# Pooled attention and a token/channel mixer in one kernel: every unit in program order on VectorE and ScalarE, with the q block transposes first in each unit

## The chip, the cores and the metric

The kernel runs on one core of one Trainium2 chip. The metric is the device time of one execution in microseconds. "The span" is the time from the first to the last instruction of the profiled execution; it is 1.7 to 1.9 us shorter than the time of the same execution.

A core has engines that run side by side, each through its own list of instructions: TensorE (PE in the profile, PEld for its weight loads), VectorE (DVE), ScalarE (ACT) and GpSimd (POOL). In the kernel before they are busy for 286.7, 178.4, 99.5 and 133.6 us of a span of 325.3. They meet at semaphores; TensorE's longest wait there for another engine is 14.4 us.

## The reference

```python
# attention over pooled keys: q, k, v are [8 batches, 8 heads, 576, 64], float32
k_p = k.reshape(B, H, 72, 8, D).mean(axis=3)        # 576 keys -> 72
v_p = v.reshape(B, H, 72, 8, D).mean(axis=3)
attn = softmax(q @ k_p.T / sqrt(D))
x = (attn @ v_p), heads side by side                # [8, 576, 512]
# mixer
h  = relu(x.T @ w_tok1) @ w_tok2                    # over the tokens, 576 -> 256 -> 576
u  = x + h.T
h2 = relu(u @ w_ch1) @ w_ch2                        # over the channels, 512 -> 1536 -> 512
return u + h2                                       # float32
```

## The kernel before

The kernel has a head (batch 0's attention) and then nine "units". Unit n runs the channel mixer of batch n on TensorE, 48 matmuls with `w_ch1` (the "ch1" phase) and 48 with `w_ch2`, and slips the attention and the token mixer of batch n+1 between them. The matmuls are a Python generator with 48 stops, called slots; a table says which step of batch n+1 is traced at which slot. Unit 8 does the leftover rows of all batches.

```python
def unit_steps(n, st):                              # 48 slots, 0.43 us of TensorE each
    for m in range(NM):                             # NM = 12, slots 0 to 23
        ps = ps_one.tile([P, 512], FP32, name="p1")
        for kk in range(4):
            nc.tensor.matmul(out=ps, lhsT=w_ch1[...], rhs=uT[:, kk, :], ...)        # L412
            if kk == 1:
                yield
        if m % 4 != 3 or n == 0:
            nc.scalar.activation(out=GT[:, m, :], in_=ps, func=AF.Relu)             # L417
        else:
            nc.vector.tensor_scalar(out=GT[:, m, :], in0=ps, ..., op0=ALU.max)      # L419
        yield
    ...                                             # slots 24 to 47: w_ch2 (L424), output o (L429)

FIRST = {1: "K0", 3: "u0", 5: "K1", 6: "u1", 8: "q0 u2", 10: "kpT0", 11: "u3", ...}          # unit 0
LATER = {0: "Q0", 1: "kpT", 3: "Q1", 6: "e0", 8: "o0", 10: "e1", 12: "o1", 14: "e2", 16: "o2",
         18: "e3", 20: "o3", 23: "av0", 25: "av1", ...}                                      # units 1 to 7
```

The steps that matter are these.

- `Q0`, `Q1`: four VectorE block transposes each of batch n+1's q (tile `qb` to `qD`, L253), from batch 2 on. They need the transfer of `qb`.
- `kpT`: eight TensorE transposes of the pooled keys and a VectorE copy to `kD` (L211).
- `e0`, `o0` to `e3`, `o3`: the scores (TensorE L271, from `qD` and `kD`) and their exponentials on ScalarE (L277).
- `av0` to `av4`: attention times v (TensorE L293), normalised by VectorE into `x` (L311); then the token mixer (L339, L354) whose results VectorE evicts into `u` (L355).

PSUM, the matmuls' output memory, is split in pools. `ps_one`, three buffers of 128 x 512 float32, serves the ch1 and ch2 tiles and the u tiles alike. A buffer is free when its tile has been evicted (the 14.4 us above are a ch1 tile that waits for the eviction of a u tile).

```python
ps_one = ctx.enter_context(tc.tile_pool(name="ps_one", bufs=3, space=bass.MemoryType.PSUM))
ps_two = ctx.enter_context(tc.tile_pool(name="ps_two", bufs=2, space=bass.MemoryType.PSUM))   # scores, av
```

Last, who decides the order. Outside `tc.manual_schedule` the framework's scheduler chooses the order of each engine's list at compile time. Inside, the engines named run in the order of tracing.

```python
with tc.manual_schedule(engines={PE, POOLE}):
    batches = [batch_steps(b) for b in range(B)]
    with tc.manual_schedule(engines={DVE, ACT}):
        ...                                        # head, loads
        unit(0, FIRST)
    for n in range(1, B + 1):                      # VectorE and ScalarE left to the scheduler
        unit(n, LATER)
```

The softmax here doesn't subtract the row's maximum and nothing guards it: scores larger than these inputs give would overflow.

Of the kernel before, what the change touches and what calls it, by code (L numbers as in the profile page):

```python
# [12 lines left out]
PE = mybir.EngineType.PE  # L13
POOLE = mybir.EngineType.Pool
DVE = mybir.EngineType.DVE
ACT = mybir.EngineType.Activation
# [3 lines left out]
def kernel(  # L20
# [14 lines left out]
    nc = tc.nc  # L35
    B, H, S, D = q.shape
    P = 128
# [25 lines left out]
    w_tok1 = singles.tile([P, 6, DT], BF16)  # L63
    w_tok2 = singles.tile([P, 2, S], BF16)
    w_tok2t = singles.tile([P, 2, 2, P], BF16)
# [6 lines left out]
    kTs = [singles.tile([P, 2, H * SP], BF16, name=f"kTs{i}") for i in range(2)]  # L72
    kps = [singles.tile([SP, H, 2, 2, D // 2], BF16, name=f"kps{i}") for i in range(2)]
# [4 lines left out]
    def load(b):  # L78
        if b >= B:
            return  # L80
        kr = raw.tile([SP, H, POOL, D], BF16, name="kr")
        vr = raw.tile([SP, H, POOL, D], BF16, name="vr")
        qb = raw.tile([P, HP, BR * D + D], BF16, name="qb")
        if b < BY_PE:
            nc.vector.memset(qb[:, :, BR * D:], 0.0)
        loaded[b] = (kr, vr, qb)

        def q_in(a0, a1):
            return q[b, 2 * a0:2 * a1].rearrange("(a l) (p r) d -> (l p) a (r d)", l=2, r=BR)

        def kv(t, src, h0, h1):
            nc.gpsimd.dma_start(out=t[:, h0:h1].rearrange("j h i d -> j h (i d)"),
                                in_=src[b, h0:h1].rearrange("h (j i) d -> j h (i d)", i=POOL))

        if b == 0:
            for a in range(2):
                nc.sync.dma_start(out=qf[:, a:a + 1, :], in_=q_in(a, a + 1))
            loaded["q23"] = q_in
            kv(kr, k, 0, HP)
            kv(kr, k, HP, H)  # L100
            make_identity(nc, ident)
            kv(vr, v, 0, HP)
            kv(vr, v, HP, H)
        else:
            kv(kr, k, 0, H)
            if b < BY_PE:
                nc.gpsimd.dma_start(out=qb[:, :, 0:BR * D], in_=q_in(0, HP))
            else:
                for ph in range(2):
                    nc.gpsimd.dma_start(  # L110
                        out=qb[ph * 64:(ph + 1) * 64, :, 0:BR * D],
                        in_=q[b].rearrange("(a l) (j u r) d -> u (l j) a (r d)", l=2, u=2, r=BR)[ph])
            kv(vr, v, 0, H)

    def load_tok():
        nc.gpsimd.dma_start(out=f2, in_=moe_w_tok2.rearrange("(c p) n -> p c n", p=P))
        w = moe_w_tok1.rearrange("(p r) n -> p r n", r=BR)
        for half in range(2):
            rows = slice(half * BP, (half + 1) * BP)
            nc.gpsimd.dma_start(out=w_tok1[rows, 0:4, :],  # L120
                                in_=w[:, 0:8, :].rearrange("p (c u) n -> p c u n", u=2)[:, :, half])
        for half in range(2):
            rows = slice(half * BP, (half + 1) * BP)
            nc.gpsimd.dma_start(out=w_tok1[rows, 4 + half, :], in_=w[:, 8, :])

    def permute_tok2():
        src = f2.rearrange("t m (p r) -> t m r p", r=BR)
        dst = w_tok2.rearrange("t m (r p) -> t m r p", p=BP)
        for m in range(2):
            nc.gpsimd.tensor_copy(out=dst[:, m], in_=src[:, m])  # L130
        for half in range(2):
            nc.gpsimd.tensor_copy(out=w_tok2t[:, :, half, half * BP:(half + 1) * BP], in_=w_tok2[:, :, 8 * BP:S])

    def load_ch1():
        for g in range(3):
            cols = slice(g * 512, (g + 1) * 512)
            nc.gpsimd.dma_start(out=w_ch1[:, :, cols], in_=moe_w_ch1[:, cols].rearrange("(c p) n -> p c n", p=P))

    def load_ch2():
        for g in range(3):  # L140
            nc.gpsimd.dma_start(out=w_ch2[:, 4 * g:4 * g + 4, :],
                                in_=moe_w_ch2[g * 512:(g + 1) * 512, :].rearrange("(c p) n -> p c n", p=P))
# [261 lines left out]
    def unit_steps(n, st):  # L404
# [16 lines left out]
        for c in range(4):  # L421
# [8 lines left out]
            for half in range(2):  # L430
# [6 lines left out]
    HEAD = """c0 c1 d8 q0 d3 q1 d7 kpool0 d2 kpT0 d2 o0 c2 e0 kpool1 o1 e1 c3 q2 kpT1 d1 q3 d1 o2 d2 e2 vpool0 o3 vpool1  # L437
              e3 d3 av1 av0 av2 d2 av3 at_0 at_2 av4 at_1 at_3 d2 at_4 X0 X1 X2 A0 A1 A2 X3 A3 d3"""
    FIRST = {1: "K0", 3: "u0", 5: "K1", 6: "u1", 8: "q0 u2", 10: "kpT0", 11: "u3", 12: "q1", 13: "o0", 14: "e0",
             16: "kpT1 V0", 17: "o1", 18: "e1", 19: "q2", 20: "o2 V1", 21: "e2", 22: "q3", 23: "o3", 24: "e3",  # L440
             25: "av0", 26: "av1", 27: "av2", 28: "av3", 29: "av4", 31: "at0", 32: "at1", 34: "U0", 35: "U1",
             36: "t0 U2", 38: "t1 U3", 39: "U4", 40: "t2", 42: "t3", 46: "t4"}
    LATER = {0: "Q0", 1: "kpT", 3: "Q1", 6: "e0", 8: "o0", 10: "e1", 12: "o1", 14: "e2", 16: "o2",
             18: "e3", 20: "o3", 23: "av0", 25: "av1", 27: "av2", 29: "av3", 31: "av4", 33: "at0", 34: "at1",
             37: "u0", 38: "u1", 39: "t0", 40: "u2", 41: "t1", 42: "u3", 43: "u4 t2", 45: "t3", 47: "t4"}
    warm = singles.tile([P, 512], BF16)

    def head(s):
        if s[0] == "d":
            ps = ps_tr.tile([P, 512], FP32, name="pt")  # L450
            for _ in range(int(s[1:])):
                nc.tensor.matmul(out=ps, lhsT=warm[:, 0:P], rhs=warm, start=True, stop=True)  # L452
        elif s[0] == "c":
            a = int(s[1:])
            if a == 1:
                for i in range(2, HP):
                    nc.scalar.dma_start(out=qf[:, i:i + 1, :], in_=loaded["q23"](i, i + 1))
            (nc.vector.tensor_copy if a % 2 else nc.scalar.copy)(out=batches[0][2]["qb"][:, a, 0:BR * D], in_=qf[:, a, :])
        else:
            batches[0][1][s]()  # L460

    def unit(n, at):
        side = {}
        if n + 1 < B:
            load(n + 2)
            batches[n + 1][0]()
            side = batches[n + 1][1]
        for i, _ in enumerate(unit_steps(n, batches[n][2] if n < B else None)):
            for s in at.get(i, "").split() if side else []:
                if (n + 1) % 2 or s not in ("u4", "t4"):  # L470
                    (batches[0][1][s] if n == 0 and s[0] == "u" else side[s.lower() if s[0] == "U" else s])()

    with tc.manual_schedule(engines={PE, POOLE}):
        batches = [batch_steps(b) for b in range(B)]
        with tc.manual_schedule(engines={DVE, ACT}):
            nc.vector.memset(warm, 0.0)
            load(0)
            nc.vector.memset(kTs[0][D:P, 0, :], 0.0)
            nc.vector.memset(kTs[0][0:D, 1, :], 0.0)
            nc.vector.memset(w_tok1[:, 4:6, :], 0.0)  # L480
            nc.vector.memset(w_tok2t, 0.0)
            load_tok()
            load_ch1()
            permute_tok2()
            load(1)
            load_ch2()
            batches[0][0]()
            for s in HEAD.split():
                head(s)
            nc.vector.memset(kTs[1][D:P, 0, :], 0.0)  # L490
            nc.vector.memset(kTs[1][0:D, 1, :], 0.0)
            for kp in kps:
                nc.vector.memset(kp, 0.0)
            unit(0, FIRST)
        for n in range(1, B + 1):
            unit(n, LATER)

# [29 lines left out]
```

## Time and profile before

The median is 327.54 us (326.58 to 327.65). The page's second part cuts the span into 40 slices of 8.1 us; a digit is the busy share in tenths, PEclk is the granted TensorE clock in tenths of full speed, and DMA is the busy share of the core's 16 transfer engines.

```profile
PE   8699503859999899899988998999999999999994
DVE  4357207999725972697269717972465166322121
PEclk9999955986999999999999999999999999999999
DMA  7999997091691977918901210121023011204114
```

The sixth slice (40.7 to 48.8 us) is empty on TensorE and on VectorE while the transfer engines are busy. The clock record has TensorE at half clock (0.50 in the windows view) from 40.7 to 57.7 us and again from 71.4 to 78.2 us. To see what that is worth, cut the span where each unit's first ch1 matmul starts. In the windows view the columns are the stretch, its length, busy time of each engine with the number of instructions, granted clock, transfer share and GB/s.

```profile
29.00:90.30 61.30, 39.62 (x231) 19.14 (x230) 41.54 (x71) 14.74 (x26) 27.66 (x27) 0.81 0.77 116
90.30:121.70 31.40, 29.68 (x195) 15.14 (x194) 20.33 (x38) 10.35 (x18) 30.38 (x28) 1.00 0.76 134
...
219.40:248.60 29.20, 29.18 (x197) 15.38 (x195) 14.34 (x28) 10.36 (x18) 0.00 (x0) 1.00 0.16 37
248.60:278.90 30.30, 30.27 (x203) 15.99 (x202) 14.90 (x29) 10.36 (x18) 0.00 (x0) 1.00 0.15 35
```

Units 5 and 6 (the last two lines) keep TensorE busy throughout: 29.2 and 30.3 us are the floor of a unit, the second with the leftover rows of two batches. Unit 0 takes 61.3. The waits of TensorE (engine, line, what it waited for; total us, times, longest) name the reason, and the waits of VectorE name the reason behind it:

```profile
PE p L412 <- DVE u L355: 14.4, 1, 14.4
PE p L293 <- DVE x L311: 7.1, 8, 1.3
PE p L339 <- DVE xt L311: 2.0, 4, 0.7
```

```profile
DVE qD L253 <- DMA qb<-in_q_dram: 15.4, 1, 15.4
```

The timeline of VectorE in unit 0 (start, us, engine, line, operation, out<-in, count, idle time before it and who ended it) shows the scene:

```profile
33.65 1.21 DVE L148 TENSOR_TENSOR t<-kr 72x1024 f32<-72x1024 bf16 x1
50.30 0.81 DVE L253 STREAM_TRANSPOSE qD<-qb 64x576 bf16<-64x576 bf16 x1 [15.44 <-DMA qb<-in_q_dram]
51.02 0.64 DVE L149 TENSOR_TENSOR t<-t 72x512 f32<-72x512 f32 x1
51.69 0.81 DVE L253 STREAM_TRANSPOSE qD<-qb 64x576 bf16<-64x576 bf16 x1
52.53 0.69 DVE L155 TENSOR_TENSOR kp<-t 72x512 bf16<-72x512 f32 x1
53.14 1.28 DVE L355 TENSOR_TENSOR u<-p,x 128x512 bf16<-128x512 f32 x2
```

A transpose of batch 2's q, which unit 1 will need, stands in unit 0 between two halves of batch 1's key pooling. Its transfer lands at 50.3 us. Everything behind it waits too, the u evictions at 53.14 included, although their inputs had been there for 14 to 17 us. TensorE's next ch1 tile finds no free buffer; its last matmuls before the hole are those of a u tile:

```profile
38.88 0.59 PE L354 MATMUL p<-AT,w_tok 128*128 128x512 bf16 x2 [0.69 <-ACT GT L417]
53.87 1.01 PE L412 MATMUL p<-uT,w_ch 128*128 128x512 bf16 x2 [14.40 <-DVE u L355]
```

In unit 2, and likewise in units 1, 3 and 4, VectorE mixes transposes of a later batch with the x evictions:

```profile
136.44 0.81 DVE L253 STREAM_TRANSPOSE qD<-qb 64x576 bf16<-64x576 bf16 x1
137.28 0.69 DVE L311 TENSOR_TENSOR x<-p,den 128x512 bf16<-128x512 f32 x1
137.89 0.20 DVE L305 RECIPROCAL den<-p 128x8 f32<-128x8 f32 x1
138.00 0.78 DVE L253 STREAM_TRANSPOSE qD<-qb 64x576 bf16<-64x576 bf16 x1
```

```profile
138.03 0.43 PE L293 MATMUL p<-vp,ex 72*128 72x65 bf16 x8 [1.29 <-DVE x L311]
```

This is the 1.29 us wait of L293 on x; there is one such in each of these units.

### The profile page before, as it was taken

Reading aid. Unit: us, or ns where it says so; the run is one execution under the profiler, and the core shown is the slowest. Engines: PE = TensorE matmul, PEld = TensorE weight load, DVE = VectorE, ACT = ScalarE, POOL = GpSimd, SP = SyncE. Lnnn points to the kernel's source line nnn. Section 1 sums busy time; section 2 is a strip of 40 time slices with the busy share of each in tenths; the row PEclk is TensorE's granted clock in tenths of the full one; section 3 lists DMA queues with packets and bytes.
Section 4 is the critical chain, followed back from the end, with each engine's and each line's share of the span. In section 5 each row is a group of like instructions: output and inputs, shape, how many; then the busy total and the mean of one; then the engine's idle time right before and its main releaser. Section 6 shows DMA issues by size and latency. Waiting matters only on the chain.

```text
span 325.3 us, 4486 instructions
## 1 busy us (share of the span) xinstructions
PE 286.7 (88%) x1796; PEld 145.9 (45%) x1796; DVE 178.4 (55%) x332; ACT 99.5 (31%) x176; POOL 133.6 (41%) x136
## 2 busy tenths in 40 slices
PE   8699503859999899899988998999999999999994
PEld 3465201434554355445544554355545554444441
DVE  4357207999725972697269717972465166322121
ACT  2453301820056007400650074007402810330500
POOL 7292200199999999967725481500000000000000
PEclk9999955986999999999999999999999999999999
DMA  7999997091691977918901210121023011204114
GB/s 152 216 206 203 207 174 110 0 144 37 100 199 22 153 160 102 149 34 128 189 0 32 67 32 0 34 64 34 0 57 75 0 34 42 57 0 97 32 34 97
DMA packets 26868, 28.25 MB, mean 87 GB/s; under 512 B 4960, under 2 KB 21728, under 8 KB 26848
## 3 DMA queue, kind: packets, MB, share of 16 engines
q0 software_dynamic: 20512, 17.35, 36.1%
q1 hardware_dynamic: 6048, 10.03, 12.4%
q10 hardware_dynamic: 288, 0.59, 0.6%
q8 instruction: 14, 0.23, 0.3%
q14 instruction: 6, 0.05, 0.0%
HBM read 35.85 MB, written 9.44 MB: 139 GB/s over the span
## 4 chain that ended last, share of the span: by engine, by line
PE 70%; DVE 19%; DMA 7%; ACT 1%; issue 1%
PE p L412 25%; PE p L424 23%; DVE qD L253 8%; DMA qb<-in_q_dram 7%; PE p L354 5%; PE p L271 4%; DVE x L311 4%; PE p L339 4%; PE pt L452 3%; PE pt L364 2%; PE p L293 1%; DVE vp L158 1%; DVE o L429 1%; DVE den L305 1%; DVE xt L311 1%
## 5 line engine op out<-in xcount | busy, mean ns | idle before, releaser
L424 PE MATMUL p<-w_ch,GT 128*128 128x512 bf16 x432 | 112.8, 383 | 0.0
L412 PE MATMUL p<-uT,w_ch 128*128 128x512 bf16 x384 | 97.1, 383 | 15.8 <-DVE u L355 14.4
L417 ACT ACTIVATE GT<-p 128x512 bf16<-128x512 f32 x84 | 49.6, 591 | 105.1 <-PE p L412 93.0
L412 PEld LDWEIGHTS <-w_ch 128*128 128x128 bf16 x432 | 41.7, 98 | 53.1 <-issue 16.6
L424 PEld LDWEIGHTS <-GT 128*128 128x128 bf16 x432 | 39.0, 98 | 39.2 <-issue 4.1
L253 DVE STREAM_TRANSPOSE qD<-qb 64x576 bf16<-64x576 bf16 x48 | 39.0, 813 | 25.2 <-DMA qb<-in_q_dram 15.4
L419 DVE TENSOR_SCALAR GT<-p 128x512 bf16<-128x512 f32 x24 | 16.4, 684 | 60.2 <-PE p L412 60.2
L277 ACT ACTIVATE ex<-p 72x576 bf16<-72x576 f32 (+1 forms) x64 | 41.2, 646 | 10.9 <-PE p L271 10.2
L149 POOL TENSOR_TENSOR t<-t 72x512 f32<-72x512 f32 x24 | 30.4, 1268 | 1.9
L429 DVE TENSOR_TENSOR o<-p,u 128x512 f32<-128x512 f32 x32 | 21.9, 686 | 10.4 <-PE p L424 10.2
L293 PE MATMUL p<-vp,ex 72*128 72x65 bf16 x320 | 17.5, 197 | 9.4 <-DVE x L311 7.1
L148 POOL TENSOR_TENSOR t<-kr 72x1024 f32<-72x1024 bf16 x12 | 25.5, 2126 | 0.1
L148 POOL TENSOR_TENSOR t<-vr 72x1024 f32<-72x1024 bf16 x12 | 25.4, 2116 | 0.0
L355 DVE TENSOR_TENSOR u<-p,x 128x512 bf16<-128x512 f32 x32 | 21.9, 688 | 6.3 <-PE p L354 6.3
L293 PEld LDWEIGHTS <-ex 72*128 72x128 bf16 x320 | 14.5, 100 | 23.5 <-DVE x L311 16.2
L330 ACT ACTIVATE AT<-p 128x512 bf16<-128x512 f32 x8 | 4.8, 597 | 66.0 <-PE p L339 63.3
L311 DVE TENSOR_TENSOR x<-p,den 128x512 bf16<-128x512 f32 x30 | 20.5, 682 | 0.7
L110 POOL DMA_DIRECT2D qb<-in_q_dram x12 | 7.6, 634 | 30.6 <-DVE qD L253 26.8
L354 PE MATMUL p<-AT,w_tok 128*128 128x512 bf16 x64 | 19.0, 379 | 0.9 <-ACT GT L417 0.9
L271 PE MATMUL p<-qD,kD 128*72 128x288 bf16 x96 | 19.6, 286 | 0.0
L158 POOL TENSOR_TENSOR vp<-t 72x256 bf16<-72x256 f32 x12 | 8.7, 725 | 22.3 <-PE p L293 21.6
L271 PEld LDWEIGHTS <-kD 128*72 128x72 bf16 x96 | 10.8, 113 | 10.6
(90 smaller groups left out, 243.9 us busy)
## 6 DMA issues: line engine op xcount, KB each, us to landing
out_dram<-o SPq DMA_DIRECT2D x72, 128.0 KB, 2.4
kr<-in_k_dram POOLq DMA_DIRECT2D x7, 576.0 KB, 9.1
vr<-in_v_dram POOLq DMA_DIRECT2D x7, 576.0 KB, 14.1
qb<-in_q_dram POOLq DMA_DIRECT2D x12, 288.0 KB, 9.6
w_ch<-in_moe_w_ch_dram POOLq DMA_DIRECT2D x6, 512.0 KB, 12.9
qf<-in_q_dram SPq DMA_DIRECT2D x2, 288.0 KB, 3.1
kr<-in_k_dram POOLq DMA_DIRECT2D x2, 288.0 KB, 7.8
vr<-in_v_dram POOLq DMA_DIRECT2D x2, 288.0 KB, 11.1
```

The lines of the kernel that those rows point to most:

```text
L148: eng.tensor_tensor(out=t4[:, 0:n], in0=t[:, hs, 0:4], in1=t[:, hs, 4:8], op=ALU.add)
L149: eng.tensor_tensor(out=t4[:, 0:n, 0:2], in0=t4[:, 0:n, 0:2], in1=t4[:, 0:n, 2:4], op=ALU.add)
L253: nc.vector.transpose(out=st["qD"][db * 64:(db + 1) * 64, 2 * g:2 * g + 2, :].rearrange("m a (r j u) -> m a r j u", u=2, r=BR)[:, :, :, :, ...
L271: nc.tensor.matmul(out=ps[0:SP, hl, 0:n], lhsT=lhsT, rhs=rhs, start=True, stop=True)
L277: nc.scalar.activation(out=dst, in_=src, func=AF.Exp, scale=scale)
L293: nc.tensor.matmul(out=halves[h // 4][:, (h % 4) * (D + 1):(h % 4 + 1) * (D + 1)], lhsT=st["ex"][:, h * S + n0:h * S + n0 + P], rhs=st["vp ...
L311: nc.vector.tensor_tensor(out=dst.rearrange("p (a h d) -> p a h d", a=2, d=D), in0=view[:, :, :, 0:D], in1=den[rows, :, :, None].broadcast ...
L354: nc.tensor.matmul(out=ps, lhsT=w, rhs=a, start=(i == 0), stop=(i == len(mms) - 1))
L412: nc.tensor.matmul(out=ps, lhsT=w_ch1[:, kk, m * P:(m + 1) * P], rhs=uT[:, kk, :], start=(kk == 0), stop=(kk == 3))
L417: nc.scalar.activation(out=GT[:, m, :], in_=ps, func=AF.Relu)
L424: nc.tensor.matmul(out=ps, lhsT=GT[:, m, c * P:(c + 1) * P], rhs=w_ch2[:, m, :], start=(m == 0), stop=(m == NM - 1))
L429: nc.vector.tensor_tensor(out=o_sb, in0=ps, in1=u_all[:, c, :], op=ALU.add)
```

## The change

The intent is to take the order of VectorE and ScalarE away from the scheduler in all units, and to fit the slots to that: the transposes of a unit's own q come first, and the scores wait behind them.

```diff
-    LATER = {0: "Q0", 1: "kpT", 3: "Q1", 6: "e0", 8: "o0", 10: "e1", 12: "o1", 14: "e2", 16: "o2",
+    LATER = {0: "Q0", 1: "kpT", 6: "Q1", 8: "e0", 10: "o0", 12: "e1", 13: "o1", 15: "e2", 17: "o2",
              18: "e3", 20: "o3", ...
-    with tc.manual_schedule(engines={PE, POOLE}):
+    with tc.manual_schedule(engines={PE, POOLE, DVE, ACT}):
         batches = [batch_steps(b) for b in range(B)]
-        with tc.manual_schedule(engines={DVE, ACT}):
-            ...                          # the same lines, one level further out
-            unit(0, FIRST)
+        ...
+        unit(0, FIRST)
         for n in range(1, B + 1):
             unit(n, LATER)
```

More of the change, by code (lines that the diff above doesn't have):

```diff
@@ L471, in unit @@
                     (batches[0][1][s] if n == 0 and s[0] == "u" else side[s.lower() if s[0] == "U" else s])()
-    with tc.manual_schedule(engines={PE, POOLE}):
+    with tc.manual_schedule(engines={PE, POOLE, DVE, ACT}):
         batches = [batch_steps(b) for b in range(B)]
-        with tc.manual_schedule(engines={DVE, ACT}):
-            nc.vector.memset(warm, 0.0)
-            load(0)
-            nc.vector.memset(kTs[0][D:P, 0, :], 0.0)
-            nc.vector.memset(kTs[0][0:D, 1, :], 0.0)
-            nc.vector.memset(w_tok1[:, 4:6, :], 0.0)
-            nc.vector.memset(w_tok2t, 0.0)
-            load_tok()
-            load_ch1()
-            permute_tok2()
-            load(1)
-            load_ch2()
-            batches[0][0]()
-            for s in HEAD.split():
-                head(s)
-            nc.vector.memset(kTs[1][D:P, 0, :], 0.0)
-            nc.vector.memset(kTs[1][0:D, 1, :], 0.0)
-            for kp in kps:
-                nc.vector.memset(kp, 0.0)
-            unit(0, FIRST)
+        nc.vector.memset(warm, 0.0)
+        load(0)
+        nc.vector.memset(kTs[0][D:P, 0, :], 0.0)
+        nc.vector.memset(kTs[0][0:D, 1, :], 0.0)
+        nc.vector.memset(w_tok1[:, 4:6, :], 0.0)
+        nc.vector.memset(w_tok2t, 0.0)
+        load_tok()
+        load_ch1()
+        permute_tok2()
+        load(1)
+        load_ch2()
+        batches[0][0]()
+        for s in HEAD.split():
+            head(s)
+        nc.vector.memset(kTs[1][D:P, 0, :], 0.0)
+        nc.vector.memset(kTs[1][0:D, 1, :], 0.0)
+        for kp in kps:
+            nc.vector.memset(kp, 0.0)
+        unit(0, FIRST)
         for n in range(1, B + 1):
```

## The prediction

> **What bounds the kernel now.** TensorE is busy 286.7 of 325.3 us (busy table), but unevenly. I cut the span at the starts of the nine units (windows view). Units 5 and 6, in which no q block is transposed, take 29.2 and 30.3 us with TensorE busy throughout: the floor. Units 1 to 4 take 2 to 3 us more each. Unit 0 takes 61.3.
>
> VectorE executes in order, and the automatic order put batch 2's transposes, needed only in unit 1, into unit 0: VectorE sat 15.4 us for the q transfer (waits: qD L253 <- DMA qb). TensorE, its small PSUM pool full of unevicted u tiles, sat 14.4 us behind it (p L412 <- DVE u L355). The granted clock then fell to half, 40.7 to 57.7 and 71.4 to 78.2 us. Thirteen transposes of 0.82 us then delayed unit 0's evictions.
> In units 1 to 4 a later batch's transposes sit among the x evictions and cost 1.29 us (p L293 <- DVE x) and up to 0.7 (p L339 <- DVE xt).
>
> **The change.** No instruction's work changes. Batch n+1's eight transposes (6.6 us) now run at the start of unit n, where VectorE had 2.4 and 3.7 us idle before GT evictions; the x phase is free of them.
>
> - Unit 0: the 14.4 us wait goes, and the half clock. By the trace's durations ScalarE (exps 0.58/0.70, q copies 0.69, GT 0.60) bounds slots 12 to 24 at about 10 us, the x evictions (0.89 each) the av phase. Unit 1 should start near 68 us, not 90.3: -22.
> - Units 1 to 4: the waits for x go, -2 to -3 each.
> - New in units 1 to 6: last o eviction, memsets, four transposes (3.3) and the kD copy (0.46) end about 4.9 us into the unit; the first score, 4.1 in, waits 0.8. Then Q1 (3.3) stands before the fourth GT eviction, which ends at 8.9. That holds one of three PSUM buffers; TensorE needs the next 6.75 in. If buffers rotate strictly, it waits 2.2 more, 3.0 per unit; if the next tile takes a buffer that ScalarE has freed, about 1.3 in all.
>
> **Sum.** 68 + six units at floor (178.5) + stalls 8 to 18 + the last two units unchanged (46.2) = 301 to 311 us of span, plus 2.2 by which the time exceeds the span. In the strict case the clock may drop too[...].
>
> I predict **306 us**, 297 to 318. Faster by over 2%: 0.93, within 2%: 0.05, slower: 0.02.
>
> **Right would be:** no VectorE wait for qb in unit 0, no 14.4 us wait of L412, unit 1 starting near 68 us, transposes directly after each unit's last o eviction, no waits of L293 on x in units 1 to 4. New: waits of L271 on kD (0.8) and, if strict, of L412 on DVE GT L419 (about 2, six times).
>
> **Wrong if:** unit 0 is held by something hidden now (a late w_ch or vr transfer); GpSimd runs late, whose vp writes may wait for memsets now at each unit's start; the clock drops in every unit.

68 + 178.5 + 8 to 18 + 46.2 comes to 301 to 311 us of span, 303 to 313 with the 2.2, and a fall of the clock was no term of it. That VectorE executes in order is what the runs show: in `e13_early_read` one copy that waits 15.5 us for its transfer holds up the u evictions behind it.

## The result, and the profile after

The changed kernel takes 297.82 us (four runs, 296.98 to 298.10), the kernel before 327.27 us (four runs). The ratio is 0.9098, 95% interval 0.9072 to 0.9124. Ratios here are the mean time of one kernel's fast runs over that of the other's in the same rounds, so not quite the ratio of the medians quoted.

```profile
PE   8789898999999999999999999999999999999993
DVE  4247956679467846786758676785588556121221
PEclk9999999999999999999999999999999999999998
```

The hole and the two stretches of half clock are gone: the mean granted clock is 0.996, before it was 0.961. In the units, TensorE's waits on VectorE shrink to one kind worth naming (those of the head stay as they were):

```profile
PE p L271 <- DVE kD L211: 2.9, 6, 0.6
...
PE p L293 <- DVE x L311: 0.3, 1, 0.3
```

The windows view, cut at the units' starts as before:

```profile
29.20:67.50 38.30, 34.76 (x232) 17.68 (x231) 26.51 (x50) 14.54 (x26) 21.48 (x21) 1.00 1.19 176
67.50:97.30 29.80, 29.18 (x195) 15.30 (x194) 20.95 (x39) 10.10 (x18) 19.80 (x19) 1.00 0.56 98
...
189.00:219.00 30.00, 29.41 (x199) 15.35 (x196) 21.12 (x39) 10.10 (x18) 13.39 (x13) 1.00 0.16 36
```

Unit by unit (us from one unit's first ch1 matmul to the next one's):

| unit | 0 | 1 | 2 | 3 | 4 | 5 | 6 | 7 and 8 |
|---|---|---|---|---|---|---|---|---|
| before | 61.3 | 31.4 | 33.0 | 31.6 | 33.0 | 29.2 | 30.3 | 46.4 |
| after | 38.2 | 29.8 | 30.9 | 29.9 | 30.9 | 30.0 | 30.9 | 46.4 |
| difference | -23.0 | -1.6 | -2.2 | -1.7 | -2.2 | +0.8 | +0.6 | 0 |

So 23.0 of the 29 us come from unit 0 and 7.5 from units 1 to 4; units 5 and 6 lose 1.3, because they now carry transposes that had been done earlier. The start of a later unit on VectorE reads as predicted:

```profile
67.68 0.69 DVE L429 TENSOR_TENSOR o<-p,u 128x512 f32<-128x512 f32 x1
...
68.62 3.25 DVE L253 STREAM_TRANSPOSE qD<-qb 64x576 bf16<-64x576 bf16 x4
71.90 0.46 DVE L211 COPY kD<-pt 128x576 bf16<-128x576 bf16 x1
72.39 3.32 DVE L253 STREAM_TRANSPOSE qD<-qb 64x576 bf16<-64x576 bf16 x4
75.75 0.69 DVE L419 TENSOR_SCALAR GT<-p 128x512 bf16<-128x512 f32 x1
```

The fourth GT eviction (75.75) ends 9.0 us into the unit; the forecast was 8.9. Yet TensorE does not wait for it:

```profile
72.41 0.44 PE L271 MATMUL p<-qD,kD 128*72 128x288 bf16 x2 [0.62 <-DVE kD L211]
...
73.80 1.03 PE L412 MATMUL p<-uT,w_ch 128*128 128x512 bf16 x4
74.66 0.41 PE L271 MATMUL p<-qD,kD 128*72 128x288 bf16 x2
74.90 0.59 PE L412 MATMUL p<-uT,w_ch 128*128 128x512 bf16 x2
...
76.69 0.38 PE L412 MATMUL p<-uT,w_ch 128*128 128x512 bf16 x1
```

The four matmuls from 73.80 on are the last two of the sixth ch1 tile and the first two of the seventh. So the seventh starts at about 74.2, 6.75 us into the unit as the prediction had it, and 1.5 us before that eviction has even begun. By the semaphores in the trace that tile waits for ScalarE, whose GT eviction of the fifth tile ran from 73.43 to 74.01. The ninth (76.69, its first matmul) is the one that waits for VectorE, and by then the eviction has ended.

### The profile page after: what moved, and what is told of

It is laid out like the page before. It is cut to its first block, busy times and chain, and to the rows that moved or that the text cites. A ratio compares the mean times of both kernels' runs of the same rounds, so it can differ in the third digit from the quotient of the medians.

```text
span 296.3 us, 4482 instructions
## 1 busy us (share of the span) xinstructions
PE 280.5 (95%) x1796; PEld 145.2 (49%) x1796; DVE 178.2 (60%) x332; ACT 97.7 (33%) x176; POOL 133.8 (45%) x136
## 4 chain that ended last, share of the span: by engine, by line
PE 81%; DVE 12%; ACT 4%; issue 1%
PE p L424 30%; PE p L412 23%; PE p L354 6%; DVE qD L253 6%; PE p L271 5%; PE p L339 5%; PE pt L452 3%; PE p L293 3%; PE pt L364 2%; DVE o L429 2%; ACT ex L277 2%; ACT GT L417 1%; DVE x L311 1%; DVE kD L211 1%; PE p L224 1%
## 5 line engine op out<-in xcount | busy, mean ns | idle before, releaser
L424 PE MATMUL p<-w_ch,GT 128*128 128x512 bf16 x432 | 111.0, 379 | 0.0
L412 PE MATMUL p<-uT,w_ch 128*128 128x512 bf16 x384 | 95.7, 379 | 1.6 <-ACT GT L417 1.6
L277 ACT ACTIVATE ex<-p 72x576 bf16<-72x576 f32 (+1 forms) x64 | 40.4, 646 | 14.8 <-PE p L271 13.8
L149 POOL TENSOR_TENSOR t<-t 72x512 f32<-72x512 f32 x24 | 30.3, 1263 | 1.9
L429 DVE TENSOR_TENSOR o<-p,u 128x512 f32<-128x512 f32 x32 | 22.0, 688 | 10.3 <-PE p L424 10.2
L293 PEld LDWEIGHTS <-ex 72*128 72x128 bf16 x320 | 15.2, 98 | 10.6 <-DVE x L311 2.2
L293 PE MATMUL p<-vp,ex 72*128 72x65 bf16 x320 | 16.9, 194 | 0.5 <-DVE x L311 0.3
L332 DVE TENSOR_SCALAR AT<-p 128x512 bf16<-128x512 f32 x8 | 5.5, 692 | 17.3 <-PE p L339 16.5
```

What stands on the lines that cost most here:

```text
L149: eng.tensor_tensor(out=t4[:, 0:n, 0:2], in0=t4[:, 0:n, 0:2], in1=t4[:, 0:n, 2:4], op=ALU.add)
L277: nc.scalar.activation(out=dst, in_=src, func=AF.Exp, scale=scale)
L293: nc.tensor.matmul(out=halves[h // 4][:, (h % 4) * (D + 1):(h % 4 + 1) * (D + 1)], lhsT=st["ex"][:, h * S + n0:h * S + n0 + P], rhs=st["vp ...
L412: nc.tensor.matmul(out=ps, lhsT=w_ch1[:, kk, m * P:(m + 1) * P], rhs=uT[:, kk, :], start=(kk == 0), stop=(kk == 3))
L424: nc.tensor.matmul(out=ps, lhsT=GT[:, m, c * P:(c + 1) * P], rhs=w_ch2[:, m, :], start=(m == 0), stop=(m == NM - 1))
L429: nc.vector.tensor_tensor(out=o_sb, in0=ps, in1=u_all[:, c, :], op=ALU.add)
```

## The experiments

With tile numbers left out, a build that leaves ScalarE to the scheduler and keeps all else of the change has the same sequence on every engine as the changed kernel; and a build with the new slots and only ScalarE in program order has the same as one with the new slots alone. Neither was run. The traces agree: ScalarE's sequence is the same in the kernel before and in `e1_order_only`, and the same in the changed kernel and in `e2_slots_only`, though in one of each pair the scheduler ordered it. So ScalarE's part of the change did nothing. Twelve runs were made, one of them of the changed kernel unedited, in three groups on three chips. All gave correct results.

### Which half of the change: order or slots

Run `e1_order_only`: the new regions, the old table.

```diff
-    LATER = {0: "Q0", 1: "kpT", 6: "Q1", 8: "e0", 10: "o0", 12: "e1", 13: "o1", 15: "e2", 17: "o2",
+    LATER = {0: "Q0", 1: "kpT", 3: "Q1", 6: "e0", 8: "o0", 10: "e1", 12: "o1", 14: "e2", 16: "o2",
```

> The change's program order with the old slots for transposes and scores; TensorE and ScalarE then run the sequence of the kernel before, only VectorE's order differs. Theory (the gain is VectorE's order): unit 0 as in the changed kernel, unit 1 starts at 67 to 68 us; the first score, two slots earlier, waits about 1.4 us for kD in each of units 1 to 6 instead of 0.5, so about 302 to 304 us. Rival (the moved slots carry the gain): close to the 327 of before.

Run `e2_slots_only`: the old regions, the new table (the reverse edit of the kernel before).

> The change's slots with the old regions: VectorE's sequence is that of the kernel before, only TensorE's and ScalarE's scores move. Theory: the 15.4 us wait of VectorE for q and the 14.4 us wait of TensorE stay, 326 to 329 us. Rival (slots carry the gain): under 315 us.

Measured: 304.45 us and ratio 0.9273 (0.9231 to 0.9316) for the order alone; 328.90 us and ratio 1.0006 (0.9961 to 1.0052) for the slots alone. In the first, unit 0 took 38.2 us, and the waits on kD grew from 2.9 to 8.0 us; in the second, the 14.4 us wait was still there (15.0). The waits of TensorE, first of the order alone, then of the slots alone:

```profile
PE p L271 <- DVE kD L211: 8.0, 6, 1.5
```

```profile
PE p L412 <- DVE u L355: 15.0, 1, 15.0
PE p L293 <- DVE x L311: 8.5, 8, 1.3
```

The theory stands. The new slots are worth nothing by themselves and about 5 us once the order is fixed: they give back part of what the new order costs, 1.3 us per unit in front of the first score. In the first of the two, TensorE and ScalarE run the same sequence as in the kernel before, so it is VectorE's order alone that carries the gain. VectorE's own sequence in that run is the changed kernel's, but for two neighbours that start together: what the new slots move is the scores.

### One instruction in the wrong place

Is unit 0's gain the wait, or the room that 6.6 us of transposes took? Run `e13_early_read` adds to the changed kernel a single small copy that nobody needs:

```diff
+            if n == 0 and i == 5:              # e14_late_read: i == 46
+                nc.vector.tensor_copy(out=scrap, in_=loaded[2][2][:, HP - 1, 0:32])
```

> The changed kernel with one extra VectorE instruction: a copy of 32 columns of batch 2's q block into a tile that nobody reads, put into unit 0 where the kernel before had its first transpose of that batch, ahead of the second u eviction. Theory (the gain of unit 0 is one instruction's place in an in-order queue, not its work): VectorE waits for the transfer until 47 to 51 us, TensorE waits 10 to 14 us behind the u evictions, the clock falls to half for at least one stretch, and the kernel takes 310 to 318 us. Rival (the 6.6 us of transposes crowded unit 0): within 1 us of the changed kernel.

> The same extra copy at the end of unit 0, when the transfer has landed. Theory: no wait, the time of the changed kernel within 0.5%. Rival (the extra instruction or its dependency costs by itself): as slow as the run before.

Measured: 314.88 us with the copy at slot 5 (ratio to the kernel before 0.9651, 0.9615 to 0.9686), 299.08 with the same copy at slot 46 (0.9188, 0.9127 to 0.9249). VectorE and TensorE at that place in the first of them:

```profile
52.07 0.17 DVE L474 COPY scrap<-qb 128x32 bf16<-128x32 bf16 x1 [15.50 <-DMA qb<-in_q_dram]
52.17 1.29 DVE L355 TENSOR_TENSOR u<-p,x 128x512 bf16<-128x512 f32 x2
```

```profile
52.92 1.01 PE L354 MATMUL p<-AT,w_tok 128*128 128x512 bf16 x2 [14.46 <-DVE u L355]
```

A copy of 0.17 us costs 15.8 us (314.88 - 299.08), because of where it stands. Unit 0 is 55.1 us with it and 38.2 without. Of the 23.0 us that the change won in unit 0, this accounts for 16.8: the wait of 14.5, and a stretch of half clock that begins in it and outlasts it, 41.2 to 58.3 us. The two matmuls in the last line take 1.01 us instead of the usual 0.59. The other 6 us of the 23.0 fit the 16 transposes that had stood in the rest of unit 0 and the second stretch of half clock; they were not separated further. The sizes were a little over what was expected (the transfer landed at 52, a wait of 14.5 against 10 to 14). The late copy was to cost under 0.5%. The medians agree with that (299.08 against 297.82), but its ratio is 1.0% above the changed kernel's 0.9098, with one execution of four at 302.5 us. The profiled execution (298.12 us) has the changed kernel's unit times to within 0.05 us, and the changed kernel itself, run again in another group, has a ratio of 0.9157; so one kernel's ratios from two groups can differ by nearly that much.

### The dose

Run `e9_ch2_later`: in the kernel before, the transfers of `w_ch2` are issued behind those of batch 2 instead of ahead of them, so that q is earlier in the same queue.

```diff
-            load_ch2()
             batches[0][0]()
 ...
             load(n + 2)
+            if n == 0:
+                load_ch2()
```

> The kernel before with the 1.5 MB of w_ch2 moved behind batch 2's transfers in the same queue; VectorE's order is that of before but for two transposes that stand a place or two earlier. Theory (VectorE waits for a transfer in its turn in a full queue): q lands about 7 us earlier, VectorE's wait falls from 15.4 to 7 to 10 us, 317 to 323 us. Rival (the wait has another cause): 327 us and a wait of 15 us.

Measured: 322.75 us, ratio 0.9875 (0.9851 to 0.9900). VectorE's wait ended at 42.4 instead of 50.3 us:

```profile
42.36 0.81 DVE L253 STREAM_TRANSPOSE qD<-qb 64x576 bf16<-64x576 bf16 x1 [10.21 <-DMA qb<-in_q_dram]
```

```profile
PE p L354 <- DVE u L355: 9.1, 1, 9.1
```

VectorE waits 10.2 instead of 15.4 us, TensorE 9.1 instead of 14.4, and the time falls by 4.1. The transfer landed 7.9 us earlier (about 7 was expected); VectorE's wait shrank by less, because in this build it also began earlier (at 32.2 instead of 34.9 us). The wait is the place of a transfer in a full queue, as the theory has it: the DMA row of the kernel before shows the transfer engines at least 90% busy from 8 to 49 us. With 1.5 MB taken out of its way q landed those 7.9 us earlier; by what rule the queue takes its transfers is not shown. The move saves far less than the 23 us of the change, since most of the wait, the transposes in unit 0 and the half clock stayed (the clock row of its page reads 5, 7 and 6 in the sixth, seventh and ninth slice).

### Unit 0 alone

Run `e5_two_units`: the kernel before with units 0 and 1 in the inner region and units 2 to 8 left to the scheduler.

```diff
             unit(0, FIRST)
-        for n in range(1, B + 1):
+            unit(1, LATER)
+        for n in range(2, B + 1):
```

> The kernel before with only units 0 and 1 in program order on VectorE and ScalarE, units 2 to 8 left to the scheduler. Theory: unit 0 falls from 61 to about 38 us; the scheduler now puts 16 transposes into the rest of unit 1, so unit 1 is no better than before, and units 2 to 4 keep their waits for x (31.6 to 33 us each): 303 to 308 us in all, so that unit 0 is three quarters of the gain. Rival (the gain is spread over all units): over 315 us.

Measured: 308.88 us, ratio 0.9455 (0.9420 to 0.9490), just over the range expected. Unit 0 takes 38.2 us, as in the changed kernel. Unit 1 takes 36.7, worse than the 31.4 of before: the scheduler moved batch 3's and batch 4's transposes into it, the x phase ran behind, and the clock fell to half for 3.4 us. Units 2 to 4 keep the times of before (33.0, 31.6, 33.0). So in both kernels in which the scheduler had the later units, it did this to the unit just before them: to unit 0 in the kernel before and, more mildly, to unit 1 here.

### Why the fourth GT eviction does no harm

The prediction had left open whether the late fourth GT eviction would stop TensorE. Run `e6_strict` hands the three buffers of `ps_one` out in strict turn: three names with one buffer each, given back in the order of the evictions as traced.

```diff
+    free, held = list("abc"), []
+    def one(shape=None, dtype=FP32):
+        slot = free.pop(0)
+        ps = ps_one.tile(shape or [P, 512], dtype, name="p1" + slot)     # ps_one: bufs=1
+        held.append((ps, slot))
+        return ps
+    def done(ps): ...                   # free.append(slot), called at the traced eviction
```

> The changed kernel with the three buffers of the small PSUM pool handed out in strict turn, in the order in which the program frees them, instead of by the scheduler. The order on every engine stays. Theory (the predicted 2.2 us wait per unit was avoided only because the seventh ch1 tile took a buffer that ScalarE had freed): TensorE now waits for the fourth GT eviction on VectorE, 1 to 2 us in each of units 1 to 6, 6 to 12 us in sum, 304 to 310 us. Rival (the fourth eviction isn't late enough to matter whatever the buffers): no such wait, 298 us.

(A first build of this experiment, which rotated by a counter and did not give buffers back in the order of eviction, deadlocked in the head.)

Measured: 315.34 us, ratio 0.9628 (0.9579 to 0.9676), against 299.20 and 0.9157 of the changed kernel on the same chip. The waits of TensorE (two of the three names):

```profile
PE p1a L433 <- DVE GT L440: 6.2, 3, 2.1
PE p1c L433 <- DVE GT L440: 6.2, 3, 2.1
```

That is 2.1 us in each of units 1 to 6, 12.4 in sum, the strict case of the prediction. The clock fell too, to half, four times for 3.4 us each in the profiled execution. Each time the first slower matmuls stand 0 to 1.1 us behind the end of such a wait: at 77.30, 176.14, 210.20 and 244.40 us, behind waits that ended at 76.20, 175.03, 210.20 and 243.72. Two of the six waits brought no fall, so the length of the wait alone does not settle it; what does is not shown. The first of the four:

```profile
76.20 0.59 PE L433 MATMUL p1a<-uT,w_ch 128*128 128x512 bf16 x2 [2.08 <-DVE GT L440]
...
77.74 1.91 PE L433 MATMUL p1b<-uT,w_ch 128*128 128x512 bf16 x4
```

(Four such matmuls take 1.03 us at full clock.) The measured time is above the range expected because the expectation had only the waits and not the clock: in the profiled execution the two units without a fall of the clock are 2.2 us longer than in the changed kernel (33.1 against 30.9, 32.2 against 29.9), and the four with one 3.9. In unit 0 the strict turn also makes TensorE wait 2.6 us for u evictions, mostly in place of other waits: that unit is 0.4 us longer. The trace has the same sequence on every engine as the changed kernel's. So the changed kernel is spared 16 us by a detail that its source does not show: the scheduler hands the seventh tile a buffer that ScalarE emptied.

### Can the wait on kD be had back?

The changed kernel has one new cost: 2.9 us of waits on kD. Run `e8_q1_behind_gt` puts the second four transposes behind the fourth GT eviction. Run `e7_late_scores` puts the first scores a slot later. Run `e11_both` does both.

```diff
 # changed:         6: "Q1", 8: "e0", 10: "o0", 12: "e1", 13: "o1", 15: "e2", 17: "o2"
 # e8_q1_behind_gt: 7: "Q1", 8: "e0", 10: "o0", 12: "e1", 13: "o1", 15: "e2", 17: "o2"
 # e7_late_scores:  6: "Q1", 9: "e0", 11: "o0", 12: "e1", 14: "o1", 16: "e2", 17: "o2"
 # e11_both:        7: "Q1", 9: "e0", 11: "o0", 12: "e1", 14: "o1", 16: "e2", 17: "o2"
```

> The changed kernel with the second four transposes one slot later, behind the fourth GT eviction; TensorE and ScalarE have the same sequence. Theory (no TensorE wait hangs on that eviction, because the next ch1 tile takes a buffer that ScalarE freed): within 0.3% of the changed kernel. Rival (the late eviction costs something hidden): 2 to 10 us faster.

> The changed kernel with the first scores one slot (0.43 us) later, so that they don't wait for kD. Theory (the 2.9 us of waits of L271 on kD are all the new order costs): those waits fall below 1 us in sum, 295.0 to 296.5 us. Rival (the wait only moves to a later score or to the av phase): same time as the changed kernel.

Measured in one group: 298.33 us (ratio 0.9099) with the transposes later, 297.94 (0.9084) with the scores later. The changed kernel was not in that group; its ratio in its own rounds is 0.9098. In the traces units 1 to 6 take 182.4 and 182.6 us, against 182.4 in the changed kernel. So neither helps. The first was expected. The second was a miss: its wait on kD is gone (0.2 us left), but another stands in its place:

```profile
PE p L412 <- DVE GT L419: 1.9, 6, 0.3
```

With the scores no longer in the way, TensorE reaches the ninth tile 0.3 us before VectorE's late eviction has freed its buffer. The late eviction was harmless only because the wait on kD hid it.

> The first scores one slot later and the second four transposes behind the fourth GT eviction, together. Alone, the later scores only turned 2.6 us of waits on kD into 1.9 us of waits of L412 on GT L419, and the later transposes alone did nothing. Theory (one slack, two claimants; both have to move): neither wait remains above 0.5 us in sum, 2 to 3 us faster than the changed kernel, ratio to it about 0.991. Rival (the wait moves once more, to the fifth score, which needs the second four transposes): the time of the changed kernel.

Control on the same chip, `after_again`, the changed kernel unedited:

> The changed kernel itself, as the control on the chip of the next three. About 298 us; the waits of L271 on kD about 2.9 us in sum.

Measured: 295.41 us (ratio 0.9032, 0.9002 to 0.9063) against 299.20 (0.9157, 0.9116 to 0.9199) for the control, and both waits are gone (0.2 us is left on kD). Units 1 to 6 take 179.8 us in sum against 182.4, so 2.6 us is what the edit gives. The rest of the difference of the medians probably lies before unit 0: in the control's profiled execution unit 0 began at 31.7 us, in that of the edit at 29.7. `e11_both` is the fastest kernel.

### Is unit 0 held by ScalarE?

Run `e12_both_gt`: as `e11_both`, with two of unit 0's twelve GT evictions on VectorE.

```diff
-            if m % 4 != 3 or n == 0:
+            if m % 4 != 3 or (n == 0 and m == 3):
```

> As the run before, and in unit 0 two of the twelve GT evictions (the eighth and the twelfth) on VectorE, which now idles 2.7 us twice in that unit, instead of ScalarE, which bounds slots 12 to 24 there. If ScalarE bounds that stretch: unit 0 is 0.6 to 1.2 us shorter. If the waits there are only q copies (L271 on qT, 1.2 us) that don't hang on the amount of ScalarE work: no change.

Measured: 296.82 us (0.9076, 0.9034 to 0.9117), no better than `e11_both`, and unit 0 takes the same 38.2 us. The waits of TensorE there are unchanged (0.8 and 0.5 us on ScalarE's q copies). ScalarE has less to do and nothing gets shorter: it is the chain TensorE transpose, ScalarE copy, TensorE score that waits, not ScalarE's load.

## Why the prediction was right or wrong, point by point

The prediction held: 297.82 us lies in its range of 297 to 318, at the edge, and faster was given 0.93. The change was 29.5 us, against 21.5 forecast. The low end of its own sum, 301 + 2.2, was already 5 us too high, so only the margin put around the sum covers the result; the mechanism of the gain was right and one term was too large (the stalls, below).

- "VectorE sat 15.4 us ... TensorE ... sat 14.4 us behind it": right, and shown as a cause by a single inserted copy (+15.8 us) and by moving the transfer (4.1 us less).
- "Unit 1 should start near 68 us": it started at 67.5.
- "ScalarE ... bounds slots 12 to 24 at about 10 us": the stretch took 9.0 us (39.5 to 48.5), but the reason was wrong. With two evictions fewer on ScalarE unit 0 did not change.
- "Thirteen transposes ... delayed unit 0's evictions": the trace has 16 after the wait, of two batches; the prediction had missed three behind the xt eviction. Nothing rested on the number.
- "Units 1 to 4 ... -2 to -3 each": measured -1.6 to -2.2 net of the new kD wait, so about -2.1 to -2.7 without it.
- "The first score waits 0.8": 0.4 to 0.6, 2.9 us in six units.
- "Stalls 8 to 18" is the term that was mis-sized. Units 1 to 6 exceed the floor of 178.5 us by 3.9 us. The prediction averaged over two ways of handing out buffers. The lenient one is what the build had, and `e6_strict` shows that the strict one costs what was forecast, 2.1 us per unit, and the clock with it in four of the six units. In the lenient case the prediction still allowed 1.3 us per unit; about 0.5 of waits was measured, because the wait on kD was shorter than forecast and the tile that got the late buffer was the ninth, which came after the eviction.
- The build of the changed kernel would have said which tile waits for which engine. Without it there was the trace: in the kernel before, batch 3's q transfer at 63.76 us was released by the end of batch 2's transposes, not by its own predecessor in turn. That is a free choice of buffers of the same kind, if in another pool, and it could have moved the estimate toward the lenient case.
- "Plus 2.2 by which the time exceeds the span": this took the median of three runs against the span of one. The profiled execution's own difference was 1.8.

Why the scheduler put those transposes where it did is not shown by any run. That it took the transfer to land earlier than it does is likely, and only argued.

## What to carry to other kernels

On VectorE, which took its instructions in order, one of them cost what everything behind it waited (a copy of 0.17 us that waited 15.5 us for its transfer made the kernel 15.8 us longer), so look first for work of a later stage that waits for a transfer in front of evictions of this one: in the timeline it is a long idle entry whose releaser is a transfer of another batch. When a schedule is fixed by hand, place such work by when its data has surely landed, then find the slack of each consumer behind it; two consumers can share one slack, and then only moving both pays. And where buffers are few, ask which engine empties the buffer that the next tile gets: with the same three buffers and the same order on every engine, that alone was worth 16 us here, the fall of the clock that it brought included. Nor need a wait for a buffer mean that there are too few of them: the waits of L293 on x (7.1 us in all) and the one of 14.4 us were TensorE lacking a free PSUM buffer, and with the same number of buffers they went down to 0.3 us and to nothing. What was missing was the eviction's turn on VectorE.
